# Attention and a mixer on one core: the first batch's steps in another written order, and U's loads in another place in the queue

## The chip, the core and the metric

The kernel runs on one core of a Trainium2 chip. The core has five engines that this text names as the profile does: PE (TensorE, matrix products; PEld is its weight load), DVE (VectorE), ACT (ScalarE), POOL (GpSimd) and SP (SyncE, which here only issues transfers). The metric is the device time of one execution in microseconds; the median of three runs of the kernel before is 574.92 us.

## What is computed

Eight batches of attention with 12 heads, 448 tokens and 64 columns per head, with an RMS norm on q and k, and behind it a mixer and a two-layer product with ReLU over 768 columns:

```python
q_n, k_n = (rmsnorm(q, g_q), rmsnorm(k, g_k))
scores = scale * np.matmul(q_n, k_n.transpose(0, 1, 3, 2))
scores = scores - np.max(scores, axis=-1, keepdims=True)
attn = np.exp(scores)
attn = attn / (np.sum(attn, axis=-1, keepdims=True) + 1e-09)
x = np.matmul(attn, v)            # then heads side by side: (8, 448, 768)
xt = x.transpose(0, 2, 1)
h = xt @ U @ V                    # U: 448 x 32, V: 32 x 448, over the tokens
u = x + h.transpose(0, 2, 1)
ch = np.maximum(u @ w_ch1, 0.0) @ w_ch2     # 768 x 3072, 3072 x 768
out = u + ch
```

All inputs and the output are float32 in HBM; the products run in bfloat16.

## The kernel before

Heads are handled in groups of four (three groups to a batch, 24 in all, counted from 0) and in pairs of two (six pairs to a batch). A group's q, k and v are loaded by SP into one of three sets of staging tiles (`qf`, `kf`, `vf`), squared, summed, turned into 1/rms, scaled to bfloat16 (`qn`, `kp`), transposed by PE and taken into `qT` and `kT`. A pair's scores are made in four steps, r = 0 to 3, each of which ACT turns into exponentials `E`; then PE multiplies `E` with v (with a column of ones for the sums), and DVE divides. From the second batch on a planner with costs and due times lays attention steps between the up products (L705, 768 columns to 3072) and down products (L752) of the batch before.

The first batch has nothing before it to hide behind. Its steps stand in a string, `FRONT`, in the order in which they are issued; each engine then works through its own instructions in that order and waits where an operand or a buffer isn't ready. The string is walked once:

```python
load_u()
load_v(2)
for step in FRONT.split():
    step, _, eng = step.partition(":")
    name, *a = step.split(".")
    steps[name](*map(int, a), engines[eng])
    if name == "val":
        load(int(a[0]) + 3)
```

The numbers of a step are group (or pair), 0 for q and 1 for k, and half; the letter after the colon is the engine (a ACT, v DVE, p POOL). The names:

- `sq`, `sm`, `rt`/`rtc`, `sc`: squares, their sums (DVE, L159 for halves, L162 for whole tiles), 1/rms (ACT), scaling. A group of the first batch can be taken by halves (two heads each).
- `turn`, `tq`, `tk`: transposes on PE (L373) and the copies of them, q with the gains (L386 on DVE), k (L392).
- `S.p.r`, `E.p.r`: scores (PE L442) and exponentials (ACT L447) of pair p. `V.p.h`, `N.p.h`: products with v (PE L512, L516) and the division (DVE L525, L526), by halves of the tokens.
- `val.g`: group g's v into bfloat16 (POOL L201, L203); behind it the loads of group g + 3 are issued.
- `prepu`, `prepv`: U and V of the mixer into bfloat16 (POOL L340, L341; L331, L333). `ms`: fills on POOL.
- `mt`, `mtc`: x times U in four pieces (PE L660) and its copy (DVE L664). `mix`, `mc`: h plus x for 128 columns in PSUM (PE L669 to L672) and its copy into `uT`.
- `u.t.d`: one of the six parts of an up product for the first four hidden tiles (PE L723).
- `w`: issues the next piece of the weights from POOL (`w1b` L293 in pieces of 4, 6, 6 and 8 blocks of 128 columns, then `w2b` L301).
- `b.n`: n filler matmuls that nothing uses (L240). `gm`, `gr`, `gains`, `pg`, `gg`: the gains of the norm.

PSUM tiles of the tag `ps` rotate through four buffers (transposes, 1/rms for DVE, fillers, products with v, mt and mix), score tiles and the L723 products through two others. SP issues in program order, and each of its loads waits until the load eight places earlier has landed, since eight semaphores go round. POOL, DVE and ACT work strictly in order.

Of the kernel before, what the change touches and what calls it, by code (L numbers as in the profile page):

```python
# [27 lines left out]
def kernel(  # L28
# [14 lines left out]
    B, H, S, D = q.shape  # L43
# [49 lines left out]
    def load_qk(gi, i, eng=None):  # L93
        b, h0, n = groups[gi]
        src = (q, k)[i][b, h0:h0 + n].rearrange("(c a) (p j) d -> (a p) c (j d)", a=2, j=NT)
        (eng or nc.sync).dma_start(staged[gi][i].rearrange("p (c j) d -> p c (j d)", c=2), src)
# [8 lines left out]
    def load_v(gi, eng=None):  # L105
        b, h0, n = groups[gi]
        t = staged[gi][2]
        toks = v[b, h0:h0 + n].rearrange("h (p j) d -> p h (j d)", j=NT)
        for i in range(2):
            (eng or nc.sync).dma_start(  # L110
                t[i * R:(i + 1) * R, :NM, :].rearrange("p (h j) d -> p h (j d)", j=NJ),
                toks[:, :, i * NJ * D:(i + 1) * NJ * D])
        for e in range(2):
            hs = slice(e, 4, 2) if gi < EARLY else slice(2 * e, 2 * e + 2)
            (eng or nc.sync).dma_start(t[e * R:(e + 1) * R, NM:, :], toks[:, hs, 2 * NJ * D:])
# [113 lines left out]
    load_v(0)  # L229
    for i in range(2):  # L230
        load_qk(2, i)
    load_v(1)

    ident = consts.tile([P, P], BF16)
    make_identity(nc, ident)
# [32 lines left out]
    gg = consts.tile([P, 2], FP32)  # L268
# [45 lines left out]
    def load_u():  # L314
        for i in range(2):
            nc.sync.dma_start(Uf[i * R:(i + 1) * R, :NJ, :], Urows[:, i * NJ:(i + 1) * NJ, :])
        nc.sync.dma_start(Uf[R:P, NJ, :], Urows[:, 2 * NJ, :])
        nc.sync.dma_start(Uf[0:R, NJ + 1, :], Urows[:, 2 * NJ, :])
        nc.sync.dma_start(Vf, moe_V.rearrange("(m r) s -> m r s", m=1).to_broadcast([NQ, rank, S]))


# [471 lines left out]
    for i, (b, pr) in enumerate(pairs):  # L793
        if b == 0:
            continue
        gi, a = divmod(i, 2)
# [85 lines left out]
    for b in range(B):  # L882
# [24 lines left out]
    mlp.extend((3.9 * w, down_end, (B - 1, cols[-1], piece), B - 1) for piece, w in enumerate((1.0, 0.67, 0.34)))  # L907

    FRONT = """
        sq.0.0.0:a gm:v sq.0.1.0:a gr b.10 sm.0.0.0 gains:p sq.0.0.1:a sm.0.1.0 pg rt.0.0.0 sq.0.1.1:p b.19 sm.0.0.1 rt.0.1.0  # L910
        sc.0.0.0:v rt.0.0.1 sc.0.1.0:p sq.1.0.0:a sm.0.1.1 turn.0.0.0 sq.1.0.1:p gg turn.0.1.0 rt.0.1.1 tq.0.0:v b.10 sq.1.1.0:a
        tk.0.0 sc.0.1.1:p sm.1.0.0 sq.1.1.1:a S.0.0 sc.0.0.1:p sm.1.1.0 E.0.0 turn.0.1.1 sm.1.1.1 S.0.1 rtc.1.0 turn.0.0.1
        sm.1.0.1 val.0 E.0.1 S.0.2 sc.1.1.0:v b.8 sc.1.0.0:v E.0.2 turn.1.1.0 tk.0.1 S.0.3 sq.2.0:p b.7 rtc.1.1 tq.0.1:v tk.1.0
        S.1.0 E.0.3 sc.1.1.1:v b.6 E.1.0 S.1.1 sq.2.1:p sm.2.0 turn.1.0.0 E.1.1 S.1.2 tq.1.0:v turn.1.1.1 E.1.2 w sm.2.1 S.1.3
        V.0.0 V.0.1 E.1.3 sc.1.0.1:p tk.1.1 S.2.0 rt.2 N.0.0 S.2.1 V.1.1 E.2.0 val.1 N.0.1 turn.1.0.1 sc.2.1:v E.2.1 S.2.2 V.1.0
        tq.1.1:v E.2.2 S.2.3 N.1.0 turn.2.1.1 w sc.2.0:v E.2.3 S.3.0 turn.2.1.0 ms E.3.0 S.3.1 tk.2.0 turn.2.0.0 E.3.1 prepv
        S.3.2 tq.2.0:v V.2.0 N.1.1 E.3.2 V.2.1 tk.2.1 S.3.3 val.2 turn.2.0.1 N.2.1 E.3.3 S.4.0 N.2.0 S.4.1 E.4.0 V.3.1 tq.2.1:v
        w V.3.0 N.3.1 E.4.1 S.4.2 prepu N.3.0 E.4.2 sq.3.0:p mt.0 S.4.3 mt.1 mtc.0 E.4.3 S.5.0 mtc.1 mix.1 w E.5.0 sm.3.0 S.5.1
        V.4.0 sq.3.1:p E.5.1 S.5.2 mc.1:v V.4.1 N.4.0 E.5.2 S.5.3 mix.3 N.4.1 mix.2 E.5.3 sm.3.1 u.0.1 mt.2 mc.2:a V.5.0 mc.3:a
        V.5.1 mtc.2 rt.3 N.5.0 u.1.1 u.0.2 u.1.2 N.5.1 mix.0 u.0.3 mt.3 mc.0:a u.1.3 mix.4 mtc.3 mix.5 mc.4:a u.0.0 u.1.0 mc.5:a  # L920
        u.2.1 u.3.1 u.2.2 u.3.2 u.2.3 u.3.3 u.2.0 u.3.0 u.0.4 u.1.4 u.0.5 u.1.5 u.2.4 u.3.4 u.2.5 u.3.5
    """
    engines = {"a": nc.scalar, "v": nc.vector, "p": pool, "": None}
    beside = uT.rearrange("p k c -> p (k c)")[:, :4 * NT * D].bitcast(FP32).rearrange("p (j d) -> p j d", d=D)
# [31 lines left out]
    def scale_by(gi, i, c, eng):  # L956
# [37 lines left out]
        "prepv": lambda eng: prep_v(),  # L994
    }
    load_u()
    load_v(2)
    for step in FRONT.split():
        step, _, eng = step.partition(":")
# [53 lines left out]
    while ia < len(att) or im < len(mlp):  # L1053
# [10 lines left out]
        if take_att:  # L1064
            c, f, a = att[ia]
# [13 lines left out]
        else:  # L1079
# [6 lines left out]
            c, f, a, _ = mlp[im]  # L1086
# [35 lines left out]
```

## Time and profile before

| | us |
|---|---|
| median of three runs | 574.92 (573.59 to 576.29) |
| the profiled execution | 576.87 |
| its span | 575.1 |
| PE busy | 565.8 (98%) |
| POOL waits for group 3's q (L143 for DMA, 2 waits up to 50 us) | 3.7, longest 2.6 |
| PE waits for POOL's copy of U (L660 for L341) | 2.6 |

The span is the profiled execution without what lies around it. A row of a timeline gives the start and the duration in us, engine, line, operation, output and inputs, the count of merged instructions, and in brackets how long the engine stood idle before it and what ended the wait. A row of the busy time by stretches gives the stretch, its length, the busy time of PE, PEld, DVE, ACT and POOL with the count of instructions, the granted clock of PE as a share of full speed, the mean share of the DMA engines and GB/s.

### The profile page before, as it was taken

The numbers are of one execution on the slowest core, as the hardware profiler recorded it, in microseconds if no ns is written. First come the engines' busy times: TensorE is split into PE (matmuls) and PEld (weight loads), VectorE is DVE, ScalarE is ACT, GpSimd is POOL, SyncE is SP. The second block draws the span as 40 slices with busy tenths as digits, with TensorE's granted clock in tenths as the row PEclk, the third lists the DMA queues.
The fourth block names the chain that finished last, engine by engine and source line by source line (L and its number), as shares of the span: only waits on it lengthen the run. The fifth ranks groups of instructions, "written<-read, shape, count | busy, mean of one in ns | idle before, by whom it ended". The sixth has DMA issues, their size and how long they took to land.

```text
span 575.1 us, 11802 instructions
## 1 busy us (share of the span) xinstructions
PE 565.8 (98%) x4878; PEld 324.9 (56%) x4878; DVE 188.6 (33%) x420; ACT 309.7 (54%) x520; POOL 203.7 (35%) x305
## 2 busy tenths in 40 slices
PE   8989999999999999999999999999999999999997
PEld 7655556555655555555555555555555555555555
DVE  5854545323334222631235321541133310410011
ACT  5956772578462975467645478267762444014300
POOL 5774684365324525325414434343531000000000
PEclk9979999999999999999999999999999999999999
DMA  8899999875435852498154845376205210320022
GB/s 236 153 241 241 246 235 178 188 160 126 117 70 152 197 124 35 83 191 211 31 133 91 197 107 131 56 183 155 34 10 110 49 28 0 71 62 0 2 56 55
DMA packets 104830, 68.22 MB, mean 119 GB/s; under 512 B 66632, under 2 KB 100936, under 8 KB 104776
## 3 DMA queue, kind: packets, MB, share of 16 engines
q1 hardware_dynamic: 95124, 57.83, 44.3%
q0 software_dynamic: 9408, 9.44, 10.0%
q8 instruction: 38, 0.62, 0.5%
q10 hardware_dynamic: 244, 0.20, 0.1%
q14 instruction: 16, 0.13, 0.1%
HBM read 52.20 MB, written 11.01 MB: 110 GB/s over the span
## 4 chain that ended last, share of the span: by engine, by line
PE 94%; DMA 4%; SPq 1%; POOL 1%; ACT 0%; issue 0%; DVE 0%; POOLq 0%
PE po L752 37%; PE ph L705 37%; PE pv L553 4%; DMA vf<-in_v_dram 2%; PE sc L476 2%; PE sl L467 2%; DMA qf<-in_q_dram 2%; PE sl L488 2%; PE pr L580 1%; PE po L739 1%; PE pv L549 1%; PE sc L442 1%; PE sc L723 1%; PE sc L638 1%; PE pu L621 1%; PE pt L365 0%
## 5 line engine op out<-in xcount | busy, mean ns | idle before, releaser
L705 PE MATMUL ph<-uT,w1b 128*128 128x448 bf16 x1128 | 223.9, 352 | 0.0
L752 PE MATMUL po<-w2b,hT 128*128 128x384 bf16 x1296 | 223.5, 326 | 0.0
L752 PEld LDWEIGHTS <-hT 128*128 128x128 bf16 x1296 | 122.8, 98 | 84.1 <-issue 7.0
L705 PEld LDWEIGHTS <-w1b 128*128 128x128 bf16 x1128 | 108.2, 98 | 97.7 <-issue 2.2
L712 ACT ACTIVATE hT<-ph 128x448 bf16<-128x448 f32 x187 | 99.8, 551 | 107.0 <-PE ph L705 106.6
L411 POOL TENSOR_SCALAR qT<-qT,gg 128x448 bf16<-128x448 bf16 x36 | 50.4, 1403 | 91.8 <-DMA qT<-qn 78.0
L469 ACT ACTIVATE E<-sl,gg 128x448 bf16<-128x448 f32 x72 | 41.7, 631 | 76.1 <-PE sl L467 75.2
L193 POOL TENSOR_TENSOR qn<-qf,rs 128x384 bf16<-128x384 f32 x36 | 29.9, 830 | 112.4 <-ACT rs L170 106.7
L480 ACT ACTIVATE E<-sc,gg 128x896 bf16<-128x896 f32 x72 | 68.9, 1020 | 0.0
L762 DVE TENSOR_TENSOR ob<-po,x 128x384 f32<-128x384 f32 x46 | 25.7, 558 | 103.7 <-PE po L752 103.0
L162 DVE TENSOR_REDUCE ssq<-sq 128x14 f32<-128x896 f32 x43 | 44.9, 1079 | 24.9 <-ACT sq L140 23.2
L557 DVE RECIPROCAL r<-pv 128x6 f32<-128x6 f32 x42 | 8.2, 196 | 125.4 <-PE pv L553 125.1
L447 ACT ACTIVATE E<-sc,gg 128x896 bf16<-128x896 f32 (+1 forms) x42 | 37.4, 952 | 6.0 <-PE sc L442 5.6
L553 PE MATMUL pv<-va,E 128*128 128x65 bf16 x756 | 35.4, 194 | 0.0
L553 PEld LDWEIGHTS <-E 128*128 128x128 bf16 x756 | 32.4, 98 | 3.2
L193 POOL TENSOR_TENSOR kp<-kf,rs 128x384 bf16<-128x384 f32 x36 | 29.9, 830 | 0.0
L549 PE MATMUL pv<-vl,E 128*128 128x130 bf16 x126 | 27.6, 219 | 0.0
L645 DVE TENSOR_TENSOR x<-sc,x 128x384 bf16<-128x384 f32 x42 | 20.8, 551 | 17.4 <-PE sc L638 17.4
L169 ACT ACTIVATE rs<-ssq,eps 128x28 f32<-128x28 f32 x21 | 6.6, 316 | 32.1 <-DVE ssq L162 32.1
L558 DVE TENSOR_TENSOR x<-pv,r 128x384 bf16<-128x384 f32 x42 | 23.4, 558 | 1.4
L489 ACT ACTIVATE E<-sl,gg 128x448 bf16<-128x448 f32 x36 | 23.3, 647 | 0.0
L201 POOL CAST va<-vf 128x768 bf16<-128x768 f32 x24 | 20.7, 864 | 2.5 <-DMA vf<-in_v_dram 2.5
(134 smaller groups left out, 435.2 us busy)
## 6 DMA issues: line engine op xcount, KB each, us to landing
qf<-in_q_dram SPq DMA_DIRECT2D x23, 448.0 KB, 3.8
kf<-in_k_dram SPq DMA_DIRECT2D x23, 448.0 KB, 5.0
vf<-in_v_dram SPq DMA_DIRECT2D x48, 192.0 KB, 5.5
out_dram<-ob SPq DMA_DIRECT2D x48, 192.0 KB, 2.7
w2b<-in_moe_w_ch_dram POOLq DMA_DIRECT2D x8, 576.0 KB, 13.3
w1b<-in_moe_w_ch_dram POOLq DMA_DIRECT2D x2, 1152.0 KB, 17.1
vf<-in_v_dram SPq DMA_DIRECT2D x48, 32.0 KB, 5.5
w1b<-in_moe_w_ch_dram POOLq DMA_DIRECT2D x1, 1536.0 KB, 23.2
```

The costliest lines, as they stand in the source:

```text
L162: nc.vector.tensor_reduce(ssqs[gi][:, i, :], sqs.pop((gi, i)), AX, ALU.add)
L193: nc.gpsimd.tensor_tensor(main.rearrange("p (t i) d -> p i t d", i=2), src[:, c, :2 * NJ].rearrange("p (i t) d -> p i t d", i=2), rs[:, c, ...
L411: nc.gpsimd.tensor_scalar(qT[:, a], qT[:, a], gg[:, 0:1], None, ALU.mult)
L447: nc.scalar.activation(es[(b, pr)][:, 2 * r:2 * r + n, :], sc[:, :n, :S], AF.Exp, scale=scal, bias=bias)
L469: nc.scalar.activation(E[:, 4 + i, :], ts[i], AF.Exp, scale=scal, bias=bias)
L480: nc.scalar.activation(E[:, 2 * r:2 * r + 2, :], tiles[r][:, :, :S], AF.Exp, scale=scal, bias=bias)
L549: nc.tensor.matmul(pv[:, i].rearrange("p e d -> p (e d)"), E[:, 2 * NJ, w:w + P], vl[:, lp, :], start=True, stop=False)
L553: nc.tensor.matmul(pv[:, i, e, :], E[:, 2 * j + e, w:w + P], va[:, (lp + 2 * e) * NJ + j, :], start=False, stop=(e == 1 and j == NJ - 1))
L705: nc.tensor.matmul(ph, w1b[:, dt, ht * P:(ht + 1) * P], uT[:, dt, off:off + S], start=(dt == 0), stop=(dt == KD - 1))
L712: nc.scalar.activation(hT[:, ht, off:off + S], ph, AF.Relu)
L752: nc.tensor.matmul(po, hT[:, ht, col:col + P], w2b[:, ht, half * HALF:(half + 1) * HALF], start=(ht == 0), stop=(ht == KH - 1))
L762: nc.vector.tensor_tensor(ob[:, h], po, urows(b, col, half), ALU.add)
```

## The change

The 203 steps of `FRONT` are put in another order, with some on other engines, and the loads that SP issues are put in another order: U's four small loads go ahead of group 1's v, and the mixer's V, which was issued with U, goes behind that v. Counted over the built kernels: 46 more filler matmuls on PE; two takes of q on ACT instead of DVE; three halves scaled by DVE instead of POOL; two halves squared by POOL instead of ACT; one copy into `uT` by DVE instead of ACT. `prepu` stands ahead of `prepv`, `val.2` and the third piece of the weights, where it stood behind them; the first piece of the weights stands directly behind `val.0`. Behind the front every engine's instructions come in the same order as before.

```diff
     load_v(0)
     for i in range(2):
         load_qk(2, i)
-    load_v(1)
...
         nc.sync.dma_start(Uf[R:P, NJ, :], Urows[:, 2 * NJ, :])
         nc.sync.dma_start(Uf[0:R, NJ + 1, :], Urows[:, 2 * NJ, :])
+
+    def load_low():
         nc.sync.dma_start(Vf, moe_V.rearrange("(m r) s -> m r s", m=1).to_broadcast([NQ, rank, S]))
...
     FRONT = """
-        sq.0.0.0:a gm:v sq.0.1.0:a gr b.10 sm.0.0.0 gains:p sq.0.0.1:a sm.0.1.0 pg rt.0.0.0 sq.0.1.1:p b.19 sm.0.0.1 rt.0.1.0
-        sc.0.0.0:v rt.0.0.1 sc.0.1.0:p sq.1.0.0:a sm.0.1.1 turn.0.0.0 sq.1.0.1:p gg turn.0.1.0 rt.0.1.1 tq.0.0:v b.10 sq.1.1.0:a
-        tk.0.0 sc.0.1.1:p sm.1.0.0 sq.1.1.1:a S.0.0 sc.0.0.1:p sm.1.1.0 E.0.0 turn.0.1.1 sm.1.1.1 S.0.1 rtc.1.0 turn.0.0.1
-        sm.1.0.1 val.0 E.0.1 S.0.2 sc.1.1.0:v b.8 sc.1.0.0:v E.0.2 turn.1.1.0 tk.0.1 S.0.3 sq.2.0:p b.7 rtc.1.1 tq.0.1:v tk.1.0
-        S.1.0 E.0.3 sc.1.1.1:v b.6 E.1.0 S.1.1 sq.2.1:p sm.2.0 turn.1.0.0 E.1.1 S.1.2 tq.1.0:v turn.1.1.1 E.1.2 w sm.2.1 S.1.3
-        V.0.0 V.0.1 E.1.3 sc.1.0.1:p tk.1.1 S.2.0 rt.2 N.0.0 S.2.1 V.1.1 E.2.0 val.1 N.0.1 turn.1.0.1 sc.2.1:v E.2.1 S.2.2 V.1.0
-        tq.1.1:v E.2.2 S.2.3 N.1.0 turn.2.1.1 w sc.2.0:v E.2.3 S.3.0 turn.2.1.0 ms E.3.0 S.3.1 tk.2.0 turn.2.0.0 E.3.1 prepv
-        S.3.2 tq.2.0:v V.2.0 N.1.1 E.3.2 V.2.1 tk.2.1 S.3.3 val.2 turn.2.0.1 N.2.1 E.3.3 S.4.0 N.2.0 S.4.1 E.4.0 V.3.1 tq.2.1:v
-        w V.3.0 N.3.1 E.4.1 S.4.2 prepu N.3.0 E.4.2 sq.3.0:p mt.0 S.4.3 mt.1 mtc.0 E.4.3 S.5.0 mtc.1 mix.1 w E.5.0 sm.3.0 S.5.1
-        V.4.0 sq.3.1:p E.5.1 S.5.2 mc.1:v V.4.1 N.4.0 E.5.2 S.5.3 mix.3 N.4.1 mix.2 E.5.3 sm.3.1 u.0.1 mt.2 mc.2:a V.5.0 mc.3:a
-        V.5.1 mtc.2 rt.3 N.5.0 u.1.1 u.0.2 u.1.2 N.5.1 mix.0 u.0.3 mt.3 mc.0:a u.1.3 mix.4 mtc.3 mix.5 mc.4:a u.0.0 u.1.0 mc.5:a
-        u.2.1 u.3.1 u.2.2 u.3.2 u.2.3 u.3.3 u.2.0 u.3.0 u.0.4 u.1.4 u.0.5 u.1.5 u.2.4 u.3.4 u.2.5 u.3.5
+        gm:v sq.0.0.0:a gr gains:p sm.0.0.0 sq.0.1.0:a ms sm.0.1.0 rt.0.0.0 pg b.20 rt.0.1.0 gg sc.0.0.0:p sc.0.1.0:v sq.0.0.1:a
+        turn.0.0.0 sm.0.0.1 turn.0.1.0 sq.0.1.1:p b.24 tk.0.0 rt.0.0.1 sm.0.1.1 tq.0.0:a sq.1.0.0:p sq.1.0.1:a sc.0.0.1:v S.0.1
+        S.0.0 rt.0.1.1 sm.1.0.1 turn.0.0.1 E.0.0 b.14 sc.0.1.1:v tq.0.1:v E.0.1 S.0.2 sq.1.1.0:p sm.1.0.0 b.8 E.0.2 S.0.3
+        sq.1.1.1:p sm.1.1.0 turn.0.1.1 b.22 E.0.3 val.0 sm.1.1.1 rtc.1.0 tk.0.1 rtc.1.1 sc.1.1.0:v S.1.1 w S.1.0 sc.1.1.1:v
+        V.0.1 E.1.0 sc.1.0.0:v turn.1.1.0 sq.2.0:p E.1.1 sc.1.0.1:v S.1.2 turn.1.0.0 N.0.1 E.1.2 S.1.3 tk.1.0 turn.1.1.1
+        sq.2.1:p sm.2.0 V.0.0 tq.1.0:a E.1.3 S.2.0 N.0.0 E.2.0 S.2.1 tk.1.1 V.1.0 sm.2.1 V.1.1 E.2.1 turn.1.0.1 S.2.2 rt.2
+        tq.1.1:v S.2.3 w b.18 E.2.2 sc.2.1:v val.1 E.2.3 S.3.0 sc.2.0:v E.3.0 S.3.1 turn.2.1.0 prepu turn.2.0.0 tk.2.0 E.3.1
+        S.3.2 N.1.1 V.2.1 w tq.2.0:v E.3.2 S.3.3 V.2.0 N.2.1 prepv turn.2.0.1 E.3.3 N.2.0 S.4.0 S.4.1 tq.2.1:v E.4.0 val.2 V.3.1
+        N.1.0 V.3.0 E.4.1 N.3.1 S.4.2 turn.2.1.1 w N.3.0 E.4.2 mt.0 tk.2.1 S.4.3 sq.3.0:p mt.1 E.4.3 S.5.0 mtc.1 S.5.1 E.5.0
+        V.4.0 mtc.0 V.4.1 sm.3.0 E.5.1 sq.3.1:p S.5.2 mix.1 E.5.2 N.4.0 mix.3 S.5.3 mc.1:v mix.2 E.5.3 mc.3:v mix.0 mc.2:a u.0.1
+        sm.3.1 V.5.0 mc.0:a V.5.1 N.4.1 u.1.1 rt.3 u.0.2 u.1.2 N.5.1 u.0.3 mt.2 u.1.3 N.5.0 u.0.0 u.1.0 u.2.1 mtc.2 u.3.1 mt.3
+        u.2.2 mix.4 mtc.3 u.3.2 u.2.3 mc.4:a mix.5 u.3.3 u.2.0 mc.5:a u.3.0 u.0.4 u.1.4 u.0.5 u.1.5 u.2.4 u.3.4 u.2.5 u.3.5
     """
...
     load_u()
+    load_v(1)
+    load_low()
     load_v(2)
```

## The prediction

> **What bounds the kernel now.** I read the page's summary and its chain first, then the busy time by stretches, then the timeline of each engine up to 46 us.
>
> ```profile
> span 575.1 us, 11802 instructions
> ...
> PE 94%; DMA 4%; SPq 1%; POOL 1%; ACT 0%; issue 0%; DVE 0%; POOLq 0%
> ```
>
> The chain that ended last is 94% TensorE (PE), so what delays PE delays the end. Behind the front, which ends with the last L723 matmul at 45.84 us, where the up products L705 begin, the order of the instructions is the same in both kernels on all five engines. So the change is worth what it does to the start of the first up product. The next rows are PE's (start, duration in us, then what the idle time before it waited for).
>
> ```profile
> 28.56 0.36 PE L442 MATMUL sc<-qT,kT 64*128 64x448 bf16 x2
> 31.55 1.04 PE L660 MATMUL pu<-x 128*128 128x256 bf16 x4 [2.62 <-POOL x L341]
> ...
> 39.12 0.22 PE L512 MATMUL pv<-vl,E 128*128 128x130 bf16 x1
> ...
> 40.11 0.73 PE L723 MATMUL sc<-uT,w1b 128*128 128x448 bf16 x3
> ...
> 41.25 0.39 PE L660 MATMUL pu<-x 128*128 128x128 bf16 x4
> 41.47 0.35 PE L723 MATMUL sc<-uT,w1b 128*128 128x448 bf16 x1
> 41.66 0.35 PE L669 MATMUL ph<-Vr,x 128*128 128x448 bf16 x1
> ...
> 42.05 0.35 PE L669 MATMUL ph<-Vr,x 128*128 128x448 bf16 x1
> ...
> 42.43 3.57 PE L723 MATMUL sc<-uT,w1b 128*128 128x448 bf16 x18
> 45.84 1.30 PE L705 MATMUL ph<-uT,w1b 128*128 128x448 bf16 x6
> ```
>
> PE stands still for 2.62 us before step mt.0, waiting for prepu on GpSimd (POOL). What that does to the clock is in the stretches (length, busy us of each engine, granted clock, DMA share, GB/s):
>
> ```profile
> 30.69:34.11 3.42, 2.56 (x11) 1.29 (x11) 0.69 (x2) 0.63 (x1) 2.29 (x4) 0.50 1.12 260
> 34.11:37.52 3.41, 3.41 (x33) 2.07 (x32) 2.39 (x5) 2.37 (x3) 2.59 (x3) 0.50 1.14 230
> 37.52:40.93 3.41, 3.41 (x60) 2.67 (x58) 2.85 (x8) 2.66 (x6) 2.15 (x4) 1.00 1.16 217
> ```
>
> The granted clock is one half for two stretches of 3.4 us, although PE was busy again from 31.55.
>
> **What goes.** POOL's rows show why prepu (L340, L341) is late:
>
> ```profile
> 13.02 0.64 POOL L203 CAST vl<-vf 64x128 bf16<-64x128 f32 x2
> ...
> 18.78 1.06 POOL L293 DMA_DIRECT2D w1b<-in_moe_w_ch_dram  x1
> ...
> 29.62 0.29 POOL L203 CAST vl<-vf 64x128 bf16<-64x128 f32 x1 [0.29 <-DMA vf<-in_v_dram]
> 30.07 0.82 POOL L293 DMA_DIRECT2D w1b<-in_moe_w_ch_dram  x1 [0.16 <-issue]
> 30.94 0.32 POOL L340 CAST Ub<-x 128x160 bf16<-128x160 f32 x1
> 31.20 0.29 POOL L341 CAST x<-x 128x128 bf16<-128x128 f32 x1
> 32.57 1.67 POOL L143 TENSOR_TENSOR sq<-qf 128x896 f32<-128x896 f32 x1 [1.08 <-DMA qf<-in_q_dram]
> ```
>
> It stands in POOL's order behind val.2, the copies of group 2's v (groups count from 0), whose last piece lands at 29.62, and behind a w1b issue. Not U's arrival: its last load was issued at 17.05 (row below), twelve us before. Now prepu stands ahead of val.2, so the 2.62 us go, and with them this half clock: from 31.55 to 37.52 PE worked without a gap at half speed, 5.97 us for 2.98 us of work. Together 5.6 us: if nothing took their place, the first up product would begin at 40.2. That is the bound of the gain.
>
> **What is late next.** Two arrivals, both on POOL, both behind SP's queue:
>
> ```profile
> 17.05 0.47 SPq L318 DMA_DIRECT2D x<-in_moe_U_dram  x1
> ```
>
> ```profile
> SPq L318 <- DMA kf<-in_k_dram: 1.6, 1, 1.6
> ```
>
> The twentieth SP load waited 1.6 us for group 2's k. In the new order the twentieth load is the last piece of group 1's v instead of U's last, and the mixer's V, group 2's v and group 3's q and k follow in the same places. So the reordering of the loads moves U, and holds group 1's v back behind four small U issues; val.1 is not hurt: its last piece leaves at 17.05 at the latest, as U's did, and POOL asks for it later than before, behind the second w1b issue. It brings none of the later loads sooner.
>
> The weights do change. The first w1b issue stands directly behind val.0, which ends at about 13.7 (last POOL row of group 0's v); I put it at 14.2 with the squares that come ahead of it, instead of 18.78. Between 16 and 20 us the DMA was nearly free, so this chunk is loaded for nothing, but the second and larger chunk is then under way while V, group 2's v and group 3's q are on their way:
>
> ```profile
> 18.00:20.00 2.00, 1.83 (x33) 1.43 (x34) 1.12 (x2) 1.53 (x4) 1.98 (x3) 1.00 0.16 17
> ...
> 24.00:26.00 2.00, 1.97 (x48) 1.48 (x45) 1.79 (x6) 2.00 (x3) 1.24 (x4) 1.00 1.19 214
> ```
>
> From 20 us on the DMA is full (214 GB/s in 24 to 26). V and group 2's v took from about 20, where the hole ends, to 29.6. The second chunk has six column blocks where the first has four, so each of its rows is half as long again; if rows of weights and of loads alternate and half the 9.6 us is the weights', they take 2.4 us more. Bounds: -1.6 (SP's wait above doesn't happen) to +2.4. The full DMA rows are nearer to the upper end: I take +2.0 for group 2's v and group 3's q.
>
> **The new wait.** With +2.0 val.2 ends at 31.9, and V.4.0, which needs it, starts there; PE has by then done mt.0, mt.1 and most of the scores. The scores themselves go at ScalarE's pace, as before. On VectorE (DVE), sm.3.0 stands directly ahead of N.4.0, mc.1 and mc.3, and it waits for sq.3.0 on POOL, which waits for group 3's q. The DVE rows of these steps before:
>
> ```profile
> 34.28 1.08 DVE L162 TENSOR_REDUCE ssq<-sq 128x14 f32<-128x896 f32 x1
> ...
> 36.67 0.18 DVE L525 RECIPROCAL r<-pv 128x4 f32<-128x4 f32 x1 [0.77 <-PE pv L516]
> 36.89 0.42 DVE L526 TENSOR_TENSOR x<-pv,r 128x256 bf16<-128x256 f32 x1
> ```
>
> sq.3.0 began at 32.57; with +2.0 it begins at 34.6 and ends at 36.2; sm.3.0 ends at 37.3, N.4.0 at 37.9. Meanwhile PE can run V.4.0 and V.4.1 (0.99 from 39.12 to 40.11), mix.1 and mix.3 (0.39 each, 41.66 to 42.05) and two score steps (an L723 matmul of the same 448 columns takes 0.19 of 41.47 to 41.66): 2.15 us, to 34.0. These fill the pool's four PSUM buffers, and mix.2 needs the one that N.4.0 frees. So PE idles from 34.0 to 37.9, 3.9 us. In the kernel before this was hidden: PE itself was late by the stall and the half clock.
>
> **The sum.** From mix.2 on PE has four mix (1.55), V.5.0 and V.5.1 (1.0), mt.2 and mt.3 (0.22 each, 41.25 to 41.47) and 24 matmuls L723 (18 take 3.41 from 42.43 to 45.84, so 4.55): 7.5 us. At full clock it would end at 45.4. But an idle time of 2.62 us gave a half clock that began 1.8 us after its start and lasted 6.83; one of 3.9 us gives at least that. Taken in the same steps it lies from 37.52 to 44.35, and PE, working from 37.9, loses half of 6.45, 3.2 us: 48.6. N.4.1 stands behind sm.3.1 as N.4.0 does behind sm.3.0; I add 0.3 for it: 48.9, against 45.84: +3.1 us. The profiled execution took 576.87 (span 575.1), so 580.0 in its terms; it was 1.95 above the median, 574.92, and I carry the difference over: 578.0.
>
> The Trainium skill, "TensorE: Matmul & The Clock Gate", section "What's actually happening", says that the clock halves after at least one idle window of about 3.4 us and is full again after one busy window. The trace differs twice: 2.62 us of idle were enough, and two stretches were slow, the second after one busy for 2.56 of 3.42 us. By the page's rule the half clock would end at 40.93: the second case below.
>
> **Without cost.** 46 more filler matmuls of 128 columns, all before about 24 us: four such take 0.22 (41.25 to 41.47), so 2.5 us. They lie where PE waits for ScalarE, which sets the pace there (busy 2.00 of 2.00 in the stretch from 24), and would cost up to 2.5 if it didn't. Two takes of q go from DVE to ScalarE and two half squares from ScalarE to POOL: nothing on balance, estimated at 0.4 either way from a DVE row of the same 128x256 kind (0.42). One mc goes from ScalarE to DVE, about 0.6 (an estimate from the 0.42 for 256 columns), behind N.4.0, while PE still works on mix.2. fill_mixer comes early on POOL, before any k or v is there to work on.
>
> **Rivals.** First, the half clock lasts one stretch: PE works throughout 37.9 to 40.93, and the row 34.11:37.52, all busy, was the last slow one. Then it loses 1.5 instead of 3.2: 47.2 with the 0.3, +1.3 us, 576.2. Loads no later than before with two slow stretches come to the same. For it: the stretch that failed to restore the clock was busy for only three quarters. Against: the only case in the trace lasted two.
>
> Second, faster: group 3's q comes sooner. SP's wait of 1.6 us for group 2's k doesn't happen, and V, group 2's v and group 3's q leave that much earlier, with the hole at 18 to 20 us already used by the weights. This decides once q lands before about 31.4, 1 us sooner than before: then N.4.0 ends at about 34.9, PE idles under 2 us, the clock stays full, and the 7.5 us from 34.9 with 0.5 for sm.3.1 end at 42.9: -2.9 us; with q at 30.8, -3.5. I price it at -3.4: 571.5. For it: the two known losses go in any case. Against: the same loads in the same places, and more weights beside them.
>
> **Chances.** The forecast 0.51, one stretch 0.23, faster 0.26. A measurement of this kernel can tell about 0.5%, 2.9 us, from no change: the forecast counts as slower, though barely, the first rival as the same. The range goes from the second rival's price, 571.5, less 0.5, to the forecast with loads at +3 and another slow stretch begun (1.0 and 1.7): 580.7. The forecast's own range is 576.5 to 580.7.
>
> **What would show it.** Right: prepu ends before 26 us and no wait L660 on L341; the first w1b issue near 14; a wait of 3 to 4 us ahead of an L669 near 38, with DVE's L162 waiting for POOL; granted clock 0.50 for two stretches after it; first L705 near 48.9. Wrong: group 3's q used by POOL before 32, no gap over 2 us between 28 and 46, or an L705 before 44.

## The result and the profile after

| | before | after |
|---|---|---|
| median, us | 574.69 (573.59 to 576.77, 6 runs) | 583.55 (582.23 to 585.04, 6 runs) |
| ratio | | 1.0149, interval 1.0122 to 1.0176 |
| the profiled execution, us | 576.87 | 584.17 |
| first up product begins at, us | 45.84 | 53.16 |

The change costs 8.9 us. The forecast was 578.0, with a range up to 580.7: the direction is right, the cost is far larger.

Page of the changed kernel, span and chain:

```profile
span 582.4 us, 11892 instructions
...
PE 92%; DMA 4%; SPq 2%; ACT 0%; DVE 0%; POOL 0%; issue 0%; POOLq 0%
```

The span is 7.3 us longer, and the first up product begins 7.3 us later: all of it is in the front, as the prediction took it. One thing about the base: the profiled execution of before, with its half clock, is not a typical one. Of 76 later executions of that kernel 8 had a mean granted clock under 0.995, as this one has with its two slow stretches (0.994; median of the 8 576.8 us), and 41 had 0.998 or more (median 574.3). So two slow stretches are not what the median has.

TensorE's timeline of the changed kernel (start, duration, what ended the idle time before; L661, L670, L706 are L660, L669, L705 of before):

```profile
29.73 0.61 PE L661 MATMUL pu<-x 128*128 128x256 bf16 x4
...
30.36 0.60 PE L661 MATMUL pu<-x 128*128 128x256 bf16 x4
30.89 0.72 PE L443 MATMUL sc<-qT,kT 64*128 64x448 bf16 x4
36.54 0.27 PE L513 MATMUL pv<-vl,E 128*128 128x130 bf16 x1 [4.93 <-POOL vl L203]
...
42.94 0.56 PE L670 MATMUL ph<-Vr,x 128*128 128x448 bf16 x1 [2.02 <-DVE x L527]
...
53.16 1.30 PE L706 MATMUL ph<-uT,w1b 128*128 128x448 bf16 x6
```

The 2.62 us wait for prepu is gone, as meant: mt.0 starts at 29.73 without one. Two waits took its place: 4.93 us for group 2's v, and 2.02 us for VectorE. POOL's timeline shows where the first comes from:

```profile
14.27 1.06 POOL L292 DMA_DIRECT2D w1b<-in_moe_w_ch_dram  x1
...
18.67 0.89 POOL L292 DMA_DIRECT2D w1b<-in_moe_w_ch_dram  x1
...
23.63 0.29 POOL L203 CAST vl<-vf 64x128 bf16<-64x128 f32 x1 [3.23 <-DMA vf<-in_v_dram]
24.89 0.29 POOL L203 CAST vl<-vf 64x128 bf16<-64x128 f32 x1 [0.98 <-DMA vf<-in_v_dram]
...
25.52 0.29 POOL L342 CAST x<-x 128x128 bf16<-128x128 f32 x1
25.75 0.82 POOL L292 DMA_DIRECT2D w1b<-in_moe_w_ch_dram  x1
...
36.20 0.29 POOL L203 CAST vl<-vf 64x128 bf16<-64x128 f32 x1 [1.06 <-DMA vf<-in_v_dram]
...
39.54 1.68 POOL L143 TENSOR_TENSOR sq<-qf 128x896 f32<-128x896 f32 x1 [2.07 <-DMA qf<-in_q_dram]
```

Group 2's v is used at 36.20 instead of 29.62 (+6.6), group 3's q at 39.54 instead of 32.57 (+7.0). The prediction said +2.0 for both. These are the rows of one execution; after_sm_late and after_fill below, whose loads and weights are the same, have v at 33.82 and 34.29 and q at 37.20 and 37.66, 4.2 to 5.1 us later than before. (Of the 3.7 us that the table of the kernel before gives to group 3's q, the 2.6 are group 4's, at 46.98; group 3's own wait is the 1.08 in the prediction's rows.) Group 1's v, which it called unhurt, holds POOL for 3.23 and 0.98 us. The second wait is the one it named, on VectorE:

```profile
41.25 1.09 DVE L162 TENSOR_REDUCE ssq<-sq 128x14 f32<-128x896 f32 x1 [9.50 <-POOL sq L143]
...
42.46 0.42 DVE L527 TENSOR_TENSOR x<-pv,r 128x256 bf16<-128x256 f32 x1
```

Busy time by stretches (length, busy us of PE, PEld, DVE, ACT, POOL, then the granted clock):

```profile
31.61:35.03 3.42, 0.00 (x1) 0.03 (x1) 0.14 (x1) 1.66 (x2) 1.01 (x2) 1.00 1.13 249
35.03:38.44 3.41, 1.90 (x30) 1.80 (x29) 0.00 (x0) 0.00 (x0) 1.22 (x3) 0.50 1.13 252
...
45.27:48.69 3.42, 3.42 (x33) 2.46 (x31) 1.38 (x5) 0.36 (x2) 2.28 (x3) 0.50 1.11 235
48.69:52.10 3.41, 3.41 (x28) 2.05 (x27) 1.58 (x3) 1.06 (x2) 1.07 (x3) 1.00 1.13 236
```

The clock is halved for four stretches, 35.03 to 48.69; two were forecast.

What the early weights do to the other queue shows in the DMA's packets from 18 to 22 us (a row gives packets, MB, and the share of 16 engines' time; q0 carries POOL's weights, q1 what SP issues), first before, then after:

```profile
q1 hardware_dynamic: 367, 0.32, 38.1%
q0 software_dynamic: 36, 0.04, 16.6%
```

```profile
q0 software_dynamic: 611, 0.62, 99.1%
q1 hardware_dynamic: 263, 0.08, 14.0%
```

Before, the weights had hardly begun in these 4 us. After, SP's queue moves 0.08 MB where it moved 0.32 (0.35 in after_w_late below, with the changed order of the loads and the weights late). It stood still in the first half: from 18 to 20 us there are 370 packets of weights and 3 of loads, from 20 to 22 us 241 and 260. No run shows why. The last piece of group 1's v, issued at 16.56, took 8.2 us to land; in after_w_late, issued at 16.53 without the early weights, it took 3.7.

From 20 us to the landing of group 3's q the DMA is full in both kernels. First before (20 to 32.43 us, 223 GB/s), then after (20 to 39.38 us, 229 GB/s):

```profile
q0 software_dynamic: 1158, 1.36, 67.1%
q1 hardware_dynamic: 1371, 1.39, 43.3%
```

```profile
q0 software_dynamic: 1785, 2.56, 75.0%
q1 hardware_dynamic: 2091, 1.84, 34.9%
```

So 1.2 MB more of weights went while SP's queue worked its way to group 3's q, and 0.45 MB more of loads. At 229 GB/s that is 7.2 us; the landing came 6.95 us later.

### The profile page after: what moved, and what is told of

Same layout as the page of the kernel before. It is cut to its first block, busy times and chain, and to the rows that moved or that the text cites. A ratio compares the mean times of both kernels' runs of the same rounds, so it can differ in the third digit from the quotient of the medians.

```text
span 582.4 us, 11892 instructions
## 1 busy us (share of the span) xinstructions
PE 569.0 (98%) x4924; PEld 327.6 (56%) x4924; DVE 189.9 (33%) x422; ACT 309.6 (53%) x518; POOL 202.2 (35%) x304
## 4 chain that ended last, share of the span: by engine, by line
PE 92%; DMA 4%; SPq 2%; ACT 0%; DVE 0%; POOL 0%; issue 0%; POOLq 0%
PE po L753 37%; PE ph L706 37%; PE pv L554 4%; DMA qf<-in_q_dram 3%; PE sc L477 2%; PE sl L468 2%; PE sl L489 2%; DMA vf<-in_v_dram 1%; PE pr L581 1%; PE po L740 1%; PE pv L550 1%; PE sc L724 1%; SPq L115 1%; PE sc L639 1%; PE sc L443 1%; SPq L110 1%
## 5 line engine op out<-in xcount | busy, mean ns | idle before, releaser
L706 PE MATMUL ph<-uT,w1b 128*128 128x448 bf16 x1128 | 223.9, 352 | 0.0
L706 PEld LDWEIGHTS <-w1b 128*128 128x128 bf16 x1128 | 108.2, 98 | 97.6 <-issue 2.2
L162 DVE TENSOR_REDUCE ssq<-sq 128x14 f32<-128x896 f32 x43 | 44.9, 1079 | 33.2 <-ACT sq L140 23.2
```

What stands on the lines that cost most here:

```text
L162: nc.vector.tensor_reduce(ssqs[gi][:, i, :], sqs.pop((gi, i)), AX, ALU.add)
L706: nc.tensor.matmul(ph, w1b[:, dt, ht * P:(ht + 1) * P], uT[:, dt, off:off + S], start=(dt == 0), stop=(dt == KD - 1))
```

## The experiments

Every kernel was timed beside the kernel before on the same chip. "First up" is the start of the first up product in its profiled execution; the last two columns are the starts of POOL's rows in it.

| kernel | median, us (runs) | ratio to before | first up | last copy of group 2's v | group 3's q squared |
|---|---|---|---|---|---|
| after | 583.55 (6) | 1.0149 | 53.16 | 36.20 | 39.54 |
| after_w_late | 575.58 (10) | 1.0005 | 46.01 | 30.0 | 33.4 |
| loads_only | 574.38 (10) | 0.9998 | 43.00 | 28.1 | 31.1 |
| prepu_early | 575.12 (10) | 1.0009 | 44.12 | 29.2 | 32.2 |
| after_fill | 585.43 (4) | 1.0178 | 50.36 | 34.3 | 37.7 |
| before_w_early | 579.31 (4) | 1.0087 | 49.22 | 33.40 | 36.7 |
| after_w3_late | 578.94 (4) | 1.0083 | 47.53 | 34.4 | 35.8 |
| after_rows_half | 577.14 (10) | 1.0040 | 45.8 | 31.1 | 33.6 |
| loads_prepu_sm | 575.67 (10) | 1.0023 | 43.69 | 26.9 | 30.1 |
| after_old_loads | 579.72 (4) | 1.0085 | 48.0 | 32.26 | 35.6 |
| after_sm_late | 581.28 (4) | 1.0114 | 50.57 | 33.8 | 37.2 |
| before_rows_half | 575.59 (12) | 1.0002 | 44.7 | 28.8 | 31.4 |
| rows_half_prepu | 574.39 (11) | 0.9993 | 42.4 | 27.2 | 30.39 |
| after_split_rows_kept | 582.27 (4) | 1.0122 | 50.4 | 33.2 | 36.7 |
| after_rows_1k | 581.46 (4) | 1.0100 | 48.1 | 30.8 | 35.8 |
| rows_1k_prepu | 585.76 (5) | 1.0183 | 53.4 | 28.4 | 31.20 |

**Which part of the change costs.** Theory W: the early weights. Rival L: the order of the loads. Two more kernels ask what prepu and the half clock are worth by themselves.

*after_w_late*: the four `w` of the changed string put back behind the POOL steps they followed before (the second behind `prepu`, which now stands directly behind `val.1`).

```diff
-val.0 ... S.1.1 w ... S.2.3 w ... V.2.1 w ... turn.2.1.1 w
+sq.2.1:p w ... prepu w ... val.2 w ... sq.3.0:p w
```

> The changed kernel with its four w1b issues put back where the kernel before has them on POOL: behind sq.2.1, behind prepu, behind val.2 and behind sq.3.0. Everything else is the changed kernel's. Theory W (the early weight pieces hold up group 2's v and group 3's q): those land near 29.5 and 32.4 us again instead of 36.1 and 39.4; V.4.0 starts near 30 and the first up product at 44 to 46 instead of 53.2, so the time falls by 7 to 9 us to about 575. Rival L (the other order of SP's loads holds them up): they land as late as in the changed kernel and the time stays near 583.

*loads_only*: the kernel before with the changed order of the loads.

```diff
-    load_v(1)                     # behind load_qk(2, i)
...
     load_u()
+    load_v(1)
+    load_low()
     load_v(2)
```

> The kernel before with the changed order of the loads alone (U's four ahead of group 1's v, the mixer's V behind it), its written order unchanged. Theory W: nothing that the path waits for moves; prepu stays behind val.2, so the wait of 2.6 us and the half clock stay, 574 to 576. Rival L: group 2's v and group 3's q land several us later, and the time is 579 to 584.

*prepu_early*: the kernel before with `prepu` directly ahead of `val.2`.

```diff
-val.2 ... w V.3.0 N.3.1 E.4.1 S.4.2 prepu
+prepu val.2 ... w V.3.0 N.3.1 E.4.1 S.4.2
```

> The kernel before with one step moved: prepu directly ahead of val.2. The prediction's bound of the gain was 5.6 us (2.6 of wait and 3.0 of half clock). Theory O (what is late next takes most of it: sm.3.0 on DVE, which waits for group 3's q, ahead of mc.1 and N.4.0): 1 to 3 us faster, 572 to 574, with a wait of PE between 33 and 37. Rival (the stall was the only thing late): 569 to 570.

*after_fill*: fillers over the two waits of the changed kernel.

```diff
-V.4.0 ... mix.2
+b.84 V.4.0 ... b.30 mix.2
```

> The changed kernel with 84 filler matmuls ahead of V.4.0 and 30 ahead of mix.2, where PE waits 4.9 and 2.0 us: the waits stay and the clock should not fall. Theory H (of the 7.3 us by which the first up product is late, some 4 to 5 are work at half clock from 36.5 to 48.7): granted clock 1.00 throughout, first up product at 47.5 to 49, 578 to 580. Rival (PE is held by waits alone, and the half clock lies beside them): no change, 583.

With the weights late the loss is gone: ratio 1.0005, interval 0.998 to 1.003, with all the other moves of the change in place. The loads alone change nothing (0.9977 to 1.0019). (In its profiled execution the wait for prepu, which was expected to stay, is missing: group 2's v comes 1.5 us sooner than in that of before, at 28.1, and prepu with it.) So of the change only the early weights cost, alone or together with something. TensorE of after_w_late keeps one wait, the one on VectorE:

```profile
36.78 0.36 PE L670 MATMUL ph<-Vr,x 128*128 128x448 bf16 x1 [2.06 <-DVE x L527]
...
46.01 1.30 PE L706 MATMUL ph<-uT,w1b 128*128 128x448 bf16 x6
```

prepu_early takes the 2.62 us wait away and gains nothing (0.9994 to 1.0023). TensorE and then VectorE show why:

```profile
35.55 0.35 PE L669 MATMUL ph<-Vr,x 128*128 128x448 bf16 x1 [2.64 <-DVE uT L678]
```

```profile
33.88 1.09 DVE L162 TENSOR_REDUCE ssq<-sq 128x14 f32<-128x896 f32 x1 [3.67 <-POOL sq L143]
```

The stall has moved to the place that the prediction named for the changed kernel: sm.3.0 on VectorE waits for group 3's q. Where the weights lie as before, group 3's q is late enough to take back what prepu gave; and two stretches of half clock were not in the median to begin with.

after_fill is inconclusive. In its profiled execution (581.35) the clock is full throughout; in its other three (585.2 to 587.1) the mean clock was 0.994. The fillers themselves stand on the path:

```profile
41.06 1.85 PE L239 MATMUL busy<-ident 128*128 128x128 bf16 x30 [1.42 <-DVE x L527]
```

After VectorE's wait 1.85 us of filler run before mix.2.

**Which weights, and with what.** Two kernels have early weights with less around them, one has the old loads, one moves VectorE's sums.

*before_w_early*: the kernel before with its `w` behind val.0, sq.2.1, val.1 and val.2.

```diff
-sq.2.1:p ... E.1.2 w ... turn.2.1.1 w ... tq.2.1:v w ... mix.1 w
+val.0 w ... sq.2.1:p w ... val.1 w ... val.2 w
```

> The kernel before with only the four early weight pieces issued as in the changed kernel: directly behind val.0, behind sq.2.1, behind val.1 and behind val.2. Theory W (the early weight pieces alone make group 2's v and group 3's q late): the issues go out near 14, 19, 22 to 26 and 35; group 2's v is complete at 33 to 36 us instead of 29.5, group 3's squares begin at 36 to 39 instead of 32.5, PE waits 4 us or more before V.4.0 or a mix step, first up product at 51 to 54, time 580 to 584. Rival (the weights cost only together with U's loads ahead of group 1's v, or with the other moved steps): group 2's v by 31, first up product at 45 to 48, time 574 to 577.

*after_w3_late*: only the third and fourth `w` of the changed string moved back.

```diff
-V.2.1 w ... turn.2.1.1 w
+val.2 w ... sq.3.0:p w
```

> The changed kernel with only the last two of the four weight pieces moved back, behind val.2 and behind sq.3.0 of group 3; the first two stay early (near 14 and 19 us). Theory W1 (the second piece, of six blocks in rows of 3 KB, that runs beside group 2's v is what costs; the third has not yet begun to move): group 2's v still complete only at 33 us or later, first up product at 50 to 53, time 580 to 584. Rival W3 (the third piece, issued at 25.75 instead of 30.07, costs): group 2's v by 31, first up product at 46 to 48, time 575 to 578.

*after_old_loads*: the changed string with the loads in the old order.

```diff
         load_qk(2, i)
+    load_v(1)
...
     load_u()
-    load_v(1)
     load_low()
     load_v(2)
```

> The changed kernel's steps with the loads in the old order (group 1's v ahead of U's four small loads). The kernel before with the four early weight issues alone lost 4.5 us, the changed kernel 8.9; this tells what the other 4.4 are. Theory I (they come from the two together: behind U's loads, group 1's v is still under way when the second weight piece starts, so val.1 waits and everything behind it on POOL and SP slides): group 1's v complete by 18 to 20 us instead of 24.8, no wait of POOL at val.1 over 0.5 us, group 2's v by 32 to 34, first up product at 48.5 to 50.5, time 578 to 581. Rival O (they come from the other steps of the new order): within 1 us of the changed kernel, 582.5 to 584.5.

*after_sm_late*: VectorE's sums of group 3 moved out of the way.

```diff
-V.4.1 sm.3.0 E.5.1 ... mc.3:v ... u.0.1 sm.3.1 ... N.4.1
+V.4.1 E.5.1 ... mc.3:v sm.3.0 ... u.0.1 ... N.4.1 sm.3.1
```

> The changed kernel with sm.3.0 moved behind mc.3 and sm.3.1 behind N.4.1 in VectorE's order: the sums no longer hold VectorE at group 3's q ahead of N.4.0. Weights and loads as in the changed kernel, so group 2's v is still complete at about 36. If the wait named in the prediction's fifth step is a loss of its own: the 2.02 us wait ahead of the mix step goes, the 4.93 us wait ahead of V.4.0 stays, the half clock lasts two or three stretches, first up product at 49.5 to 51.5, time 580 to 582. If the late group 2's v and what is made of it set the end anyway: within 1 us of the changed kernel, 582.5 to 584.5.

The early weights alone cost 1.0087 (1.0055 to 1.0119): 4.5 us, half the loss and just under the time that theory W gave. TensorE's wait is 7.33 us there and stands at prepu, which still follows val.2:

```profile
35.32 1.03 PE L660 MATMUL pu<-x 128*128 128x256 bf16 x4 [7.33 <-POOL x L341]
```

The old loads under the changed string give nearly the same, 1.0085 (1.0058 to 1.0111). So the other half, 3.8 us from 579.72 to 583.55, is the two together: with weights late the load order costs nothing, with weights early it does. POOL of after_old_loads:

```profile
20.21 0.66 POOL L203 CAST vl<-vf 64x128 bf16<-64x128 f32 x2
...
32.26 0.29 POOL L203 CAST vl<-vf 64x128 bf16<-64x128 f32 x1 [0.85 <-DMA vf<-in_v_dram]
```

There group 1's v is in place when POOL asks (20.21, no wait, where the changed kernel waits to 24.89): its four transfers have landed by 18.3, and U's small ones run beside the weights instead (the last lands at 21.7). Theory I holds; the first up product came half a microsecond sooner than its range.

after_w3_late lies between its two theories, as it should if both are half right: moving the third and fourth piece back is worth 4.6 us of the loss (583.55 to 578.94; the third, issued at 25.75 in the changed kernel, goes at 34.69 here), the first two 3.4 (to 575.58). Group 2's v is still late, at 34.4, but group 3's q follows 1.4 us behind it instead of 3.3.

after_sm_late is 2.3 us below the changed kernel, in the range of the step's own theory, but the intervals of the two ratios overlap (1.0087 to 1.0141 and 1.0122 to 1.0176). The 2.02 us ahead of the mix step are gone; 2.56 came back later, ahead of another piece of mt:

```profile
34.17 0.22 PE L513 MATMUL pv<-vl,E 128*128 128x130 bf16 x1 [2.75 <-POOL vl L203]
...
40.60 0.27 PE L661 MATMUL pu<-x 128*128 128x128 bf16 x2 [1.10 <-DVE x L527]
...
44.38 0.58 PE L661 MATMUL pu<-x 128*128 128x128 bf16 x4 [2.56 <-DVE x L527]
```

The waits on VectorE are longer here, 1.10 and 2.56 against 2.02; the first up product comes 2.6 us sooner, and group 2's v, with the same loads, 2.4 us sooner (33.82 against 36.20). So these rows do not show that VectorE's order was a loss of its own.

**Why they cost: the length of the weights' rows.** The same bytes, in the same places, in other rows.

*after_rows_half*: each piece of six or eight blocks as two transfers of half the columns.

```diff
+        cuts = (lo, hi) if hi - lo == 4 else (lo, (lo + hi) // 2, hi)
+        for lo, hi in zip(cuts, cuts[1:]):
-        nc.gpsimd.dma_start(w1b[:, :, lo * P:hi * P], ...)
+            nc.gpsimd.dma_start(w1b[:, :, lo * P:hi * P], ...)
```

> The changed kernel with each weight piece of more than four blocks issued as two transfers of half the columns each, one directly behind the other: the same bytes at the same places, in rows of 1.5 KB (pieces of six blocks) and 2 KB (of eight) instead of 3 and 4 KB. POOL pays about 1 us more for each second issue. Theory R (rows of weights and rows of loads alternate, so longer rows take a larger share of the DMA): group 2's v complete by 31 to 33 instead of 36.1, first up product at 47 to 50, time 577 to 580. Rival Q (what counts is how many bytes of weights are queued ahead, not the length of their rows): no change, first up product within 1 us of 53.2, time 582 to 586.

*after_split_rows_kept*: cut in two as well, but between row groups, so that the rows keep their length.

```diff
+        for a, b in zip(cuts, cuts[1:]):     # (0, 6), or 0, 3, 6
-        nc.gpsimd.dma_start(w1b[:, :, lo * P:hi * P], ...)
+            nc.gpsimd.dma_start(w1b[:, a:b, lo * P:hi * P], ...)
```

> The changed kernel with each weight piece of more than four blocks issued as two transfers, like the kernel with rows of half the length (577.14 us), but cut across the other axis: each transfer holds three of the six row groups, so the rows keep their 3 KB (pieces of six blocks) and 4 KB. Same number of transfers, same bytes, same places. Theory R (the length of the weight rows sets how long the loads beside them take): group 2's v complete at 33 to 36, first up product at 50 to 53, time 580.5 to 584.5. Rival C (cutting a piece in two transfers is what helped, by its later second issue or by the queue turning between transfers): group 2's v by 32, first up product at 45 to 48, time 576 to 579.

*after_rows_1k*: every piece in transfers of two blocks.

```diff
+        for c in range(lo, hi, 2):
-        nc.gpsimd.dma_start(w1b[:, :, lo * P:hi * P], ...)
+            nc.gpsimd.dma_start(w1b[:, :, c * P:(c + 2) * P], ...)
```

> The changed kernel with every weight piece cut into transfers of two blocks of 128 columns: rows of 1 KB throughout, instead of 2, 3, 3 and 4 KB; the same bytes from the same steps, POOL pays 0.8 to 1 us for each further issue. Theory R: group 2's v complete at 28 to 30.5 (31.0 with rows of 1.5 KB, 36.1 with 3 KB), first up product at 43.5 to 46, time 574 to 577. Rival Q (no more to gain below 1.5 KB, or the extra issues on POOL take it back): as with 1.5 KB or later, first up product at 46 or more, time 577 to 580.

Half the row takes 6.4 of the 8.9 us away (1.0040, interval 1.0023 to 1.0057); the cut alone leaves 1.0122 (1.0101 to 1.0142). So it is the rows' length and not the cutting. The packets from 22 to 30 us, in the order: after, after_split_rows_kept, after_rows_half, after_rows_1k. (The profile counts bytes as they are written, in bfloat16: a row of six blocks, 3 KB of float32, is a packet of 1.5 KB.)

```profile
q0 software_dynamic: 707, 1.06, 75.5%
q1 hardware_dynamic: 808, 0.68, 31.4%
```

```profile
q0 software_dynamic: 693, 1.04, 74.2%
q1 hardware_dynamic: 781, 0.74, 40.3%
```

```profile
q0 software_dynamic: 983, 0.75, 61.2%
q1 hardware_dynamic: 1242, 1.22, 59.0%
```

```profile
q1 hardware_dynamic: 1274, 1.29, 74.5%
q0 software_dynamic: 1008, 0.51, 46.2%
```

In each the weights have 79 to 89 packets for every 100 of the loads, and the sum of bytes differs little (1.74 to 1.97 MB); in the kernel before, with rows of 2 and 3 KB in that stretch, it is 924 packets to 894. So in this stretch the two queues take turns by packets, and the one with the longer rows gets the bytes. With half the rows, 1.40 MB of weights go from 20 us to the landing of group 3's q instead of 2.56, beside the same 1.8 MB of loads, and it lands 6.0 us sooner, at 33.39. A weight packet takes 137 ns with the long rows (75.5% of 16 x 8 us, over 707), 80 and 59 ns with the shorter ones. The Trainium skill, "DMA: Bandwidth & Descriptors", section "Queues, rings and completion order", says that each DMA engine goes round between the queues it has work for, a packet at a time; these counts agree, those from 18 to 20 us do not show it.

after_rows_1k brought the loads a little sooner still (0.51 MB of weights, 1.29 MB of loads; group 3's q landed at 32.3, against 33.4 with the half rows) but was slower than the half rows and above both ranges. POOL tells why:

```profile
31.03 2.47 POOL L293 DMA_DIRECT2D w1b<-in_moe_w_ch_dram  x3
...
34.92 0.82 POOL L293 DMA_DIRECT2D w1b<-in_moe_w_ch_dram  x1 [1.42 <-DMA w1b<-in_moe_w_ch_dram]
35.80 1.67 POOL L143 TENSOR_TENSOR sq<-qf 128x896 f32<-128x896 f32 x1
```

Four issues where there was one, the last of which (POOL's twelfth) waits until the fourth weight transfer has landed at 34.63, stand ahead of group 3's squares, whose q had come.

**A version that beats both.** Four kernels from the one before, with the pieces that had helped.

*loads_prepu_sm*: loads_only and prepu_early together, with `sm.3.0` behind `N.4.1`.

```diff
-val.2 ... prepu ... sm.3.0 S.5.1 V.4.0 ... N.4.1
+prepu val.2 ... S.5.1 V.4.0 ... N.4.1 sm.3.0
```

> The kernel before with the new order of the loads, with prepu directly ahead of val.2, and with sm.3.0 moved behind N.4.1 in VectorE's order (weights at their old places). If the wait that took the place of prepu's was VectorE's order alone (sm.3.0 waiting for group 3's squares ahead of N.4.0), both known losses go: no PE wait over 1.5 us between 28 and 46, full clock there, first up product at 40.5 to 42.5, time 570 to 572.5. If the arrival of group 2's v itself sets it, PE waits 1.5 to 3 us before V.4.0 or mix.2, first up product at 43 to 44.5, time 573 to 576.

*before_rows_half*: only the half rows. *rows_half_prepu*: with `prepu` ahead of `val.2`. *rows_1k_prepu*: that with rows of two blocks (the diffs above).

> The kernel before with each weight piece of more than four blocks issued as two transfers of half the columns each (rows of 1.5 and 2 KB instead of 3 and 4 KB), everything else as it was. Theory R (a row of weights beside the loads takes by its length): group 2's v complete 1 to 2 us sooner than 29.5, group 3's squares 1.5 to 3 us sooner than 32.5; but prepu stands behind val.2 and now behind two weight issues (0.8 us more), so it comes at most 1 us sooner: time 573.5 to 575.5. Rival Q (bytes only): loads as before, prepu 0.8 us later, time 575 to 577.

> The same with prepu directly ahead of val.2. With the rows of 3 KB this order gained nothing, since VectorE then waited for group 3's squares ahead of N.4.0 and PE stood for 2.64 us. Theory R: group 3's q arrives 1.5 to 3 us sooner, that wait falls to 1 us or less, first up product at 41.5 to 43, time 571.5 to 573.5, faster than both kernels. Rival Q: as with the long rows, first up product near 44, time 574.5 to 576.

> The kernel before with prepu directly ahead of val.2 and every weight piece in transfers with rows of 1 KB. With rows of 1.5 KB this was 574.39 (ratio 0.9993), first up product at 42.4 in its profile. Theory R: group 2's v and group 3's q another 1 us sooner (26 and 29), wait ahead of the mix steps under 0.5 us, first up product at 41 to 42, time 572 to 573.5. Rival P (POOL's extra issues, some 0.9 us each and eight of them ahead of 36 us, take it back): first up product at 42.5 to 44, time 574 to 576.

None beats the kernel before. In loads_prepu_sm a wait of 1.72 us turns up ahead of mt, behind sm.3.1, which waits 1.67 us for the squares of group 3's k (1.0023, interval 1.0002 to 1.0043). before_rows_half is even (0.9979 to 1.0025): its loads came 1 us sooner, its prepu did not. rows_half_prepu went furthest:

```profile
33.77 0.35 PE L671 MATMUL ph<-Vr,x 128*128 128x448 bf16 x1 [1.08 <-DVE uT L680]
```

Its wait fell from 2.64 to 1.08 us and its clock was full, first up at 42.4 as theory R said; but its median is 0.9993 of before (0.9976 to 1.0011), so no gain that the runs can tell: the loads did as theory R said, the time did not. Against an execution of before with full clock the room is small: 574.3 less 1.8 around the span and 529.2 behind the start of the first up product (span less first up, in both kernels) puts that start at about 43.3.

rows_1k_prepu lost 10.6 us, though group 3's q landed at 28.9, where theory R had 29. POOL, which at its issues took the q up only at 31.20:

```profile
32.83 1.72 POOL L294 DMA_DIRECT2D w1b<-in_moe_w_ch_dram  x2
38.10 0.82 POOL L294 DMA_DIRECT2D w1b<-in_moe_w_ch_dram  x1 [3.56 <-DMA w1b<-in_moe_w_ch_dram]
42.70 0.82 POOL L294 DMA_DIRECT2D w1b<-in_moe_w_ch_dram  x1 [3.78 <-DMA w1b<-in_moe_w_ch_dram]
43.53 1.69 POOL L143 TENSOR_TENSOR sq<-kf 128x896 f32<-128x896 f32 x1
```

Two weight issues wait 3.56 and 3.78 us for earlier weight transfers: POOL's eleventh and twelfth, for the third and fourth, which land at 37.81 and 42.41. That is eight places earlier, the same round that holds SP's loads. Group 3's k is squared behind them; VectorE waits for these squares, and TensorE stands for 9.10 us. Rival P had the engine right, but priced the issues alone and not these waits.

## Why the prediction was right and wrong

- **prepu**: right. It ends at 25.81 and nothing waits for it. That the gain could be 5.6 us was a bound from one execution; prepu_early shows a gain of nothing in the median, since the wait moves to VectorE and two stretches of half clock were rare (8 executions of 76).
- **The loads' order "brings none of the later loads sooner"**: in the profile of loads_only they come 1.5 us sooner, in that of after_w_late no sooner (30.0 and 33.4); the time is the same in both. **"val.1 is not hurt"**: wrong, 3.23 and 0.98 us. The step compared issue times of SP's queue and did not ask what ran beside those transfers; with the early weights they took until 24.8. With the weights early, this order costs 3.8 us (after_old_loads).
- **First w1b issue at 14.2, "this chunk is loaded for nothing"**: the time is right (14.27), and 0.54 MB of weights had gone by 20 us. The price set on it is the step that failed: +2.0 for group 2's v and group 3's q, with bounds -1.6 to +2.4, measured +6.6 and +7.0 (+4.2 to +5.1 in after_sm_late and after_fill). The prediction let weights and loads take turns, which holds from 22 us on, but its sum has only the longer rows of the second piece. It left out that more weights go ahead of group 3's q: 2.56 MB from 20 us on instead of 1.36, through a DMA that was already full. The third piece, issued at 25.75 instead of 30.07, is a part of that which the sum put at nothing; after_w3_late, with the third and fourth later still, is 4.6 us faster.
- **V.4.0 at 31.9**: the mechanism is right, the time late by 4.6. The wait of 4.93 us for group 2's v stands where the forecast had TensorE at work.
- **sm.3.0 on VectorE for group 3's q**: right, by name and place, with a wait of 2.02 us. What it costs by itself after_sm_late doesn't tell.
- **The sum from there**: with the measured restart at 42.94, the 7.5 us of work end at 50.4 at full clock; the half clock to 48.69 takes half of 5.75, 2.9: 53.3, against 53.16. So the later steps hold, and the miss of 4.2 us in the profiled execution (580.0 against 584.17) is the loads' term carried through them. The other 1.3 us of the miss in the medians are the 1.95 us by which the profiled execution of before lay above its median: the prediction carried them over, and the changed kernel's lies 0.62 above.
- **The half clock**: four stretches for two. It began in the same way, during or behind an idle time, and ended behind the first stretch in which TensorE had no gap (3.42 of 3.42). The Trainium skill, "TensorE: Matmul & The Clock Gate", section "What's actually happening", has the clock halved after an idle window of about 3.4 us and full after a busy one. Here both agree: 0.00 busy in 31.61 to 35.03, and full from 48.69. The forecast took the two stretches of before as a duration; they were one with a gap and one without, so the second of the two differences that it saw from the page is none. The first stays: 2.62 us of idle were enough there.
- **Fillers and moved engines without cost**: right on balance. All of them are in after_w_late, at 1.0005 (0.998 to 1.003).
- **The rivals**: the faster one needed q before 31.4, and it came at 39.4; the one with a single slow stretch needed TensorE at work throughout that stretch, and it had gaps (1.90 us busy of 3.41).

What stays open: why SP's queue moved next to nothing from 18 to 20 us. It is not what decides: in after_sm_late and after_fill SP's queue had moved 4.03 and 3.98 MB by 22 us, almost the 4.05 of before (3.75 in the changed kernel), and group 2's v was still 4.2 and 4.7 us late. What the waits and the half clock cost apart from each other was not separated. What after_fill would have given without its own filler on the path was not tried either.

## What to carry to other kernels

A transfer put into an idle stretch of the DMA is not free: price what it still has to move when the next loads begin, and count by packets, since the queue with the longer rows takes the bytes. Before a stall is priced as a gain, look for the next arrival on the same path; here most versions that removed one wait met group 3's q or k a few microseconds later. Shorter rows for a background transfer help the loads beside it, up to the point where the extra issues, and their waits for earlier ones, hold up the engine that makes them.

## What was not expected of the hardware

- From 22 to 30 us the two queues shared by packets, not by bytes: 0.68 MB of loads in 8 us beside weight rows of 3 KB, 1.22 MB beside rows of 1.5 KB, with the weights' packets at 0.87 and 0.79 of the loads'.
- The turns do not hold at all times: 370 packets of weights and 3 of loads from 18 to 20 us in the changed kernel. No run shows why.
- More issues cost more than their own time where semaphores go round: 3.56 and 3.78 us of waiting for the transfer eight places earlier in rows_1k_prepu and 1.42 in after_rows_1k. Each of them ends as that transfer lands, so it looks like the program's round of eight and not a limit of the chip; the changed kernel's four issues show no such wait.
- The half clock lasted until a stretch in which TensorE had no gap was over: 6.83 us in before, 13.65 in after, 3.41 in after_w_late. An idle time of 2.62 us brought it on in before; one of 2.64 us in prepu_early did not.
